# A sliding-window attention backward with a gated MLP: buffers of probability pairs, and six more transposes on TensorE

## The chip, the cores and the metric

The kernel runs on one core of one Trainium2 chip. The metric is the device time of one execution in microseconds (us). A core has TensorE (PE, with its weight loads PEld), VectorE (DVE), ScalarE (ACT), GpSimd (POOL) and SyncE (SP), which here only issues DMAs. Each engine works through its own instructions in order; an instruction waits until the semaphores that it names have been raised. SP's DMAs are issued in order too: one that waits holds up all behind it.

## The reference

The kernel computes a forward pass and the gradients of one layer that mixes two branches by a gate. Cut to what matters (S = 2048 tokens, D = 512, 32 heads of 16, a window of 256 tokens, F = 1376, all bf16):

```python
g = sigmoid((x * gate_w).sum(-1, keepdims=True))
# a: attention, each query sees itself and the 255 tokens before it
scores = einsum("bhqd,bhkd->bhqk", q, k) * Dh ** -0.5     # masked to the window
a = einsum("bhqk,bhkd->bhqd", softmax(scores), v) -> @ wo
# b: gated MLP
b = einsum("bsf,fd->bsd", relu(x @ W_gate) * (x @ W_up), W_down)
out = g * a + (1 - g) * b
# returned: out and the gradients of (out * grad_out).sum() by
# A_x, A_wqkv, A_wo, B_W_gate, B_W_up, B_W_down, gate_w
```

(In the reference `x` of both branches is `A_x`.) For the attention's gradients every score tile is needed twice: as probabilities P, and as P times dP, where dP is the product of the output's gradient with V. Both are needed with keys along the partitions (as they come from the matmul) and with queries along them (transposed).

## The kernel before

The program has three stages.

**MLP, 0 to about 250 us** (lines 186 to 454). The gate's and the MLP's products, forward and backward, in tiles of 128 hidden units by 512 tokens; the results that are needed later are stored to DRAM.

**Attention, about 250 to 775 us** (lines 456 to 897). Heads are worked in four head groups `c` of eight heads (DC = 4), queries in 16 blocks `j` of 128 (NT = 16). A query block meets up to three key blocks: its own (role "d", diagonal, masked above the diagonal), the one before (role "m", middle, no mask) and the one before that (role "f", far, masked). Each meeting is made for two halves of four heads, so a block has six units, and fewer at the start of a head group: two in block 0, four in block 1. The order of the units in a whole block is m, f, d of the first half, then m, d, f of the second (lines 592 to 605). 360 units in all.

One unit goes through these steps, by slot `n` of a loop that issues one unit per slot (lines 809 to 897):

- slot n, `front`: TensorE makes the scores ST (line 616), ScalarE their exponential into Pu (line 627), POOL masks it where the role is d or f (lines 629 and 632). `front_dp`: TensorE makes dPT (line 641).
- slot n+1, `gradp`: VectorE multiplies Pu by dPT into Pd (line 646).
- slot n+2, `flip`, for units with `u.dma` set: a DMA transpose on SP's queue. The two halves of a diagonal pair share one tile PPd (Pu and Pd of both halves, 4 KB per partition), transposed in one DMA into `p2d` (line 671), which is issued two slots after the second half. A first middle unit has a tile PPm of its own (2 KB), transposed into `p2` (line 678).
- slot n+3 (LAG = 3), `rowsum`: TensorE sums rows and the products with K and V into BA (lines 655 and 657), which ScalarE copies out after the block's last unit (line 661). Then `flip` for the other units (second middle and far ones): TensorE transposes Pu and Pd in eight pieces (line 687), and a copy takes them out of PSUM, by ScalarE and VectorE in turn (`copier`, `evac`, lines 72 and 74).
- Some slots after a block's end: `small_ops` (lines 692 to 726), a division on VectorE and eight small operations on POOL; and later still `cd_piece` (lines 478 to 490), which uses the transposed tiles as weights for the gradients of K and V.

All of ST, dPT and the projections' results rotate through four PSUM tiles of one tag "M". PPd has two buffers, PPm three, Pu and Pd (of units that are flipped on TensorE) three each. A buffer of PPd or PPm is free again when its DMA transpose has landed and its `rowsum` is done.

Besides its own work the loop spreads background work by a planner with a running credit: the projections of the next group of four blocks (`project_parts`), among them `tr_rows`, a DMA transpose on SP's queue into one of two buffers `rows` (line 171), whose former content is read last by POOL's small operations (lines 709 to 716); the loads of the masked layout `z` (line 468); the weight gradients of the head group before (line 572); and in the last groups the loads and transposes of the weights of the last stage (`plan`, lines 517 and 527), all on SP's queue. A unit that is flipped on TensorE takes 0.44 from the credit (line 863).

**Output, from about 775 us on** (lines 907 to 1003). For each of 16 token blocks the output, the gradient of x and pieces of other gradients, from operands that are loaded from DRAM in eight groups of two blocks.

Of the kernel before, what the change touches and what calls it, by code (L numbers as in the profile page):

```python
# [11 lines left out]
BF = mybir.dt.bfloat16  # L12
# [10 lines left out]
def kernel(  # L23
# [21 lines left out]
    P = 128  # L45
# [10 lines left out]
    DC = D // P  # L56
# [55 lines left out]
    if True:  # L112
        HH = HG // 2
# [74 lines left out]
    with ExitStack() as p1, tc.manual_schedule():  # L188
# [33 lines left out]
        half = TPG // 2  # L222
# [234 lines left out]
    if True:  # L457
# [4 lines left out]
        wk = p3b.enter_context(tc.tile_pool(name="attw", bufs=2))  # L462
# [130 lines left out]
        for c in range(DC):  # L593
            for j in range(NT):
                kbs = [k for k in (j - 1, j, j - 2) if k >= 0]
                for half in range(2):
                    order = kbs if half or len(kbs) < 3 else [kbs[0], kbs[2], kbs[1]]
                    for ki, kb in enumerate(order):
                        u = Unit()
                        u.c, u.j, u.kb, u.half = c, j, kb, half  # L600
                        u.first = ki == 0 and half == 0
                        u.last = ki == len(kbs) - 1 and half == 1
                        u.role = ("d", "m", "f")[j - kb]
                        u.dma = u.role == "d" or (u.role == "m" and half == 0)
                        units.append(u)
        NU = len(units)

        pairs = {}

        def front(u):  # L610
            tg, jl = u.j // TPG, u.j % TPG
            z = zt[(u.c * NTG + tg) % ZB]
            KTt = proj[(u.c, u.kb // TPG)][f"K{u.half}"]
            ksl = slice((u.kb % TPG) * P, (u.kb % TPG + 1) * P)
            ST = ps.tile([P, HH, P], F32, tag="M", bufs=4, name="ST")
            nc.tensor.matmul(ST[:], lhsT=KTt[:, ksl], rhs=z[:, 0, jl, :, :], start=True, stop=True)  # L616
            if u.role == "d":
                if u.half == 0:
                    pairs[(u.c, u.j)] = wk.tile([P, 2, 2, HH, P], BF, tag="PPd", bufs=2, name="PPd")
                u.PP = pairs[(u.c, u.j)][:, u.half, :, :, :]  # L620
                u.Pu, u.Pd = u.PP[:, 0, :, :], u.PP[:, 1, :, :]
            elif u.dma:
                u.PP = wk.tile([P, 2, HH, P], BF, tag="PPm", bufs=3, name="PPm")
                u.Pu, u.Pd = u.PP[:, 0, :, :], u.PP[:, 1, :, :]
            else:
                u.Pu = wk.tile([P, HH, P], BF, tag="Pu", bufs=3, name="Pu")
            nc.scalar.activation(u.Pu[:], ST[:], ACT.Exp)  # L627
            if u.role == "d":
                nc.gpsimd.affine_select(out=u.Pu[:], in_=u.Pu[:], compare_op=ALU.is_ge, fill=0.0, base=0,  # L629
                                        pattern=[[0, HH], [1, P]], channel_multiplier=-1)  # L630
            elif u.role == "f":
                nc.gpsimd.affine_select(out=u.Pu[:], in_=u.Pu[:], compare_op=ALU.is_ge, fill=0.0, base=-1,  # L632
                                        pattern=[[0, HH], [-1, P]], channel_multiplier=1)
# [147 lines left out]
        with tc.manual_schedule():  # L781
# [27 lines left out]
            while n <= NU + LAG or ev or cdq or bgq:  # L809
                now = ev.pop(n, [])  # L810
                u = units[n] if n < NU else None
# [3 lines left out]
                if u is not None:  # L815
                    gi = u.c * NTG + u.j // TPG
                    if u.first and u.j == 0:
                        sts[u.c] = st.tile([P, NT, 4, P], BF, tag="rows_st", name="rows_st")
                    if u.first and u.j % TPG == 0:
                        if gi + 1 < len(groups):  # L820
                            prq = project_parts(*groups[gi + 1])
                            due = n + sum(2 * min(3, j + 1) for j in range(u.j, u.j + TPG)) - 3
                            if gi + 2 == len(groups):
                                due -= 10
                    if u.first and u.j == 6 and u.c > 0:
                        ev.setdefault(n + 1, []).append(("dma", lambda c=u.c - 1: spill(c, NT // 2)))
                    if u.first and u.j == 1 and u.c > 0:
                        ready = grad_parts(u.c - 1)
                    if u.first and u.j == TPG - 1 and u.c > 0:
                        bgq += ready  # L830
                    front(u)
                    if u.last and gi + 1 == len(groups) and u.j % TPG in (1, 3):
                        ev.setdefault(n + 2, []).append(("dma", lambda i=(u.j % TPG) // 2: early_f(i)))
# [200 lines left out]
```

## Time and profile before

| what | us |
|---|---|
| median of 3 runs | 970.24 |
| lowest and highest | 968.97, 972.31 |
| the profiled execution, its own time | 972.45 |
| its span, first to last instruction | 970.7 |
| mean granted TensorE clock | 0.987 of full |

The page gives the busy time of each engine, a strip of the span in 40 slices and a chain of waits that ended last. A row of the timeline gives an instruction's start in us from the span's start, its length, engine, line, operation, tiles written and read, shapes, and in brackets the idle time of the engine before it with what ended that idle time. "SPq" rows are DMA issues on SP's queue: start, and how long the issue occupied the queue; the transfer lands later. A row of the waits reads: who waited, for whom, total us, number of times, longest.

### The profile page before, as it was taken

The numbers are of one execution on the slowest core, as the hardware profiler recorded it, in microseconds if no ns is written. First come the engines' busy times: TensorE is split into PE (matmuls) and PEld (weight loads), VectorE is DVE, ScalarE is ACT, GpSimd is POOL, SyncE is SP. The second block draws the span as 40 slices with busy tenths as digits, with TensorE's granted clock in tenths as the row PEclk, the third lists the DMA queues.
The fourth block names the chain that finished last, engine by engine and source line by source line (L and its number), as shares of the span: only waits on it lengthen the run. The fifth ranks groups of instructions, "written<-read, shape, count | busy, mean of one in ns | idle before, by whom it ended". The sixth has DMA issues, their size and how long they took to land.

```text
span 970.7 us, 26875 instructions
## 1 busy us (share of the span) xinstructions
PE 928.5 (96%) x11017; PEld 588.2 (61%) x11017; DVE 501.0 (52%) x918; ACT 456.6 (47%) x792; POOL 487.0 (50%) x935
## 2 busy tenths in 40 slices
PE   8999999999899998999998999989998999999998
PEld 5555655656567765677765777756776644444443
DVE  4443334334477776567765676756676322223223
ACT  5423222223367876667775667756676410000001
POOL 2644545444267766656766567765676511112211
PEclk9999999999999999999998999989999999999999
DMA  9988989998578985698969879979999899777751
GB/s 295 185 195 180 200 190 211 206 223 199 118 125 136 152 156 106 114 166 129 163 109 131 161 112 183 140 133 158 170 168 197 172 244 233 193 188 192 187 104 45
DMA packets 477172, 161.86 MB, mean 167 GB/s; under 512 B 405784, under 2 KB 474744, under 8 KB 477048
## 3 DMA queue, kind: packets, MB, share of 16 engines
q1 hardware_dynamic: 454648, 137.06, 76.2%
q10 hardware_dynamic: 20592, 17.84, 6.5%
q0 software_dynamic: 1808, 5.24, 1.6%
q8 instruction: 86, 1.41, 0.6%
q14 instruction: 38, 0.31, 0.1%
HBM read 32.15 MB, written 36.31 MB: 71 GB/s over the span
## 4 chain that ended last, share of the span: by engine, by line
PE 69%; DMA 10%; POOL 7%; DVE 6%; ACT 3%; issue 3%; SPq 1%; POOLq 0%; ACTq 0%; DVEq 0%
PE dxps L976 7%; PE wps L371 6%; PE ST L616 6%; PE pt L687 5%; PE dPT L641 5%; PE wps L572 4%; PE dxps L991 4%; DMA p2d<-PPd 4%; PE pp L128 4%; PE bps L945 3%; PE dhps L324 3%; PE dps L373 3%; PE ups L324 3%; PE gps L324 3%; PE BA L655 3%
## 5 line engine op out<-in xcount | busy, mean ns | idle before, releaser
L641 PE MATMUL dPT<-z,V 128*128 128x512 bf16 x360 | 138.6, 385 | 13.9 <-ACT PPd L627 10.8
L646 DVE TENSOR_TENSOR Pd<-Pu,dPT 128x512 bf16<-128x512 bf16 x172 | 116.7, 679 | 64.4 <-POOL Pu L632 51.1
L616 PE MATMUL ST<-z,K 128*128 128x512 bf16 x360 | 138.4, 384 | 8.0 <-ACT PPd L627 2.5
L627 ACT ACTIVATE Pu<-ST 128x512 bf16<-128x512 f32 x172 | 104.1, 605 | 47.5 <-PE ST L616 39.5
L629 POOL TENSOR_SCALAR_AFFINE_SELECT PPd<-PPd 128x512 bf16<-128x512 bf16 x128 | 81.6, 637 | 85.9 <-ACT PPd L627 85.5
L646 DVE TENSOR_TENSOR PPd<-PPd,dPT 128x512 bf16<-128x512 bf16 x128 | 87.5, 683 | 56.5 <-POOL PPd L629 55.0
L338 POOL TENSOR_TENSOR hT<-rg,upm 128x512 bf16<-128x512 bf16 x44 | 51.4, 1167 | 118.7 <-DVE upm L336 82.6
L371 PE MATMUL wps<-dgu_r,x_r 128*128 128x256 bf16 x704 | 105.6, 273 | 0.9 <-DVE wst L74 0.9
L627 ACT ACTIVATE PPd<-ST 128x512 bf16<-128x512 f32 x128 | 77.1, 602 | 51.3 <-PE ST L616 28.9
L72 ACT COPY p<-pt 128x1024 bf16<-128x1024 bf16 x86 | 87.6, 1019 | 4.8 <-PE pt L687 2.4
L371 PEld LDWEIGHTS <-x_r 128*128 128x128 bf16 x704 | 68.8, 98 | 32.2 <-issue 1.4
L632 POOL TENSOR_SCALAR_AFFINE_SELECT Pu<-Pu 128x512 bf16<-128x512 bf16 x112 | 71.4, 638 | 27.7 <-ACT Pu L627 27.4
L954 ACT COPY a_sb<-aps 128x512 f32<-128x512 f32 x16 | 9.4, 586 | 154.9 <-issue 139.7
L336 DVE SCALAR_TENSOR_TENSOR upm<-rg,ups 128x512 bf16<-128x512 bf16 x44 | 30.2, 686 | 81.7 <-ACT rg L330 42.1
L486 PE MATMUL CD<-rq,p 128*128 128x32 bf16 x928 | 68.4, 177 | 0.0
L330 ACT ACTIVATE rg<-gps 128x512 bf16<-128x512 f32 x44 | 26.3, 598 | 88.8 <-PE gps L324 43.0
L687 PE MATMUL pt<-ident,Pd 128*128 128x128 bf16 x688 | 67.8, 222 | 0.0
L687 PE MATMUL pt<-ident,Pu 128*128 128x128 bf16 x688 | 67.2, 220 | 0.0
L489 PEld LDWEIGHTS <-p 128*128 128x128 bf16 x928 | 54.8, 96 | 20.2 <-issue 1.1
L373 PE MATMUL dps<-db_r,h_r 128*128 128x512 bf16 x176 | 66.7, 379 | 0.0
L489 PE MATMUL CD<-rq,p 128*128 128x16 bf16 x928 | 66.7, 169 | 0.0
L486 PEld LDWEIGHTS <-p 128*128 128x128 bf16 x928 | 62.1, 96 | 1.2 <-issue 1.1
(167 smaller groups left out, 2250.4 us busy)
## 6 DMA issues: line engine op xcount, KB each, us to landing
dqkvo_d<-rows_st SPq DMA_DIRECT2D x7, 1024.0 KB, 6.3
hT_d<-hT ACTq DMA_DIRECT2D x44, 128.0 KB, 2.6
dgT_d<-dgu ACTq DMA_DIRECT2D x44, 128.0 KB, 3.0
duT_d<-dgu ACTq DMA_DIRECT2D x44, 128.0 KB, 3.1
duT_g<-duT_d SPq DMA_DIRECT2D x8, 640.0 KB, 5.7
gt<-hT_d SPq DMA_DIRECT2D x7, 640.0 KB, 5.8
dgT_g<-dgT_d SPq DMA_DIRECT2D x7, 640.0 KB, 5.0
z<-zT SPq DMA_DIRECT2D x60, 64.0 KB, 2.2
```

The source lines that it names most:

```text
L72: nc.scalar.copy(out, in_)
L324: nc.tensor.matmul(out[:], lhsT=w(c), rhs=x(c), start=(c == 0), stop=(c == DC - 1))
L371: nc.tensor.matmul(acc["w"][:, c, :], lhsT=x_r[:, t, c * P:(c + 1) * P], rhs=k.dgu_r[:, :, i, :], start=(go_ and c % 2 == 0), stop=no_, sk ...
L373: nc.tensor.matmul(acc["d"][:], lhsT=k.h_r[:, i, :], rhs=db_r[:, t, :], start=go_, stop=no_)
L486: nc.tensor.matmul(cd[0][:, h, :], lhsT=p2[:, 0, hh, :], rhs=rq[:, h, 0:2 * Dh], start=cd[1], stop=True, skip_group_check=True)
L489: nc.tensor.matmul(cd[0][:, h, 0:Dh], lhsT=p2[:, 1, hh, :], rhs=rq[:, h, 2 * Dh:3 * Dh], start=False, stop=True, skip_group_check=True)
L616: nc.tensor.matmul(ST[:], lhsT=KTt[:, ksl], rhs=z[:, 0, jl, :, :], start=True, stop=True)
L627: nc.scalar.activation(u.Pu[:], ST[:], ACT.Exp)
L629: nc.gpsimd.affine_select(out=u.Pu[:], in_=u.Pu[:], compare_op=ALU.is_ge, fill=0.0, base=0, pattern=[[0, HH], [1, P]], channel_multiplier=-1)
L641: nc.tensor.matmul(u.dPT[:], lhsT=VTt[:, ksl], rhs=z[:, 1, jl, :, :], start=True, stop=True)
L646: nc.vector.tensor_tensor(out=u.Pd[:], in0=u.Pu[:], in1=u.dPT[:], op=ALU.mult)
L687: nc.tensor.transpose(pt[:, a, hh, :], src[:, hh, :], ident[:])
```

## The change

Three edits. PPd gets a third buffer (4 KB more per partition). PPm gets two buffers instead of three (2 KB less). And the first middle units of the last head group, in blocks 10 to 15, no longer have `u.dma` set: these six units are flipped on TensorE, one slot later, with their Pu and Pd in the tiles of the tags Pu and Pd and not in PPm.

```diff
@@ -601,7 +601,7 @@
                         u.first = ki == 0 and half == 0
                         u.last = ki == len(kbs) - 1 and half == 1
                         u.role = ("d", "m", "f")[j - kb]
-                        u.dma = u.role == "d" or (u.role == "m" and half == 0)
+                        u.dma = u.role == "d" or (u.role == "m" and half == 0 and (c < DC - 1 or j < 10))
                         units.append(u)
@@ -616,11 +616,11 @@
             if u.role == "d":
                 if u.half == 0:
-                    pairs[(u.c, u.j)] = wk.tile([P, 2, 2, HH, P], BF, tag="PPd", bufs=2, name="PPd")
+                    pairs[(u.c, u.j)] = wk.tile([P, 2, 2, HH, P], BF, tag="PPd", bufs=3, name="PPd")
                 u.PP = pairs[(u.c, u.j)][:, u.half, :, :, :]
                 u.Pu, u.Pd = u.PP[:, 0, :, :], u.PP[:, 1, :, :]
             elif u.dma:
-                u.PP = wk.tile([P, 2, HH, P], BF, tag="PPm", bufs=3, name="PPm")
+                u.PP = wk.tile([P, 2, HH, P], BF, tag="PPm", bufs=2, name="PPm")
                 u.Pu, u.Pd = u.PP[:, 0, :, :], u.PP[:, 1, :, :]
```

## The prediction

> **What bounds the kernel now.** I read the page first: which engine is full, and what the chain of waits runs through.
>
> ```profile
> span 970.7 us, 26875 instructions
> ...
> PE 928.5 (96%) x11017; PEld 588.2 (61%) x11017; DVE 501.0 (52%) x918; ACT 456.6 (47%) x792; POOL 487.0 (50%) x935
> ...
> PE   8999999999899998999998999989998999999998
> ...
> PE 69%; DMA 10%; POOL 7%; DVE 6%; ACT 3%; issue 3%; SPq 1%; POOLq 0%; ACTq 0%; DVEq 0%
> ```
>
> TensorE is busy for 96% of the span, and in nearly every slice of it (a digit is a fortieth, in tenths), so the time can only fall where it idles or runs slowly, and every instruction added to it counts. One foreign thing stands on the chain, the DMA `p2d<-PPd`, the transpose of a diagonal pair. The view of waits says what it holds up (columns: total us, times, longest):
>
> ```profile
> ACT PPd L627 <- DMA p2d<-PPd: 19.1, 8, 4.0
> ...
> PE dPT L641 <- ACT PPd L627: 10.8, 6, 3.8
> PE ST L616 <- ACT PPd L627: 2.5, 2, 2.1
> PE dPT L641 <- DVE Pd L646: 2.3, 2, 1.4
> PE BA L655 <- ACT BAs L661: 2.2, 1, 2.2
> ```
>
> ScalarE's exponential into PPd waits until the transpose out of that buffer has landed, because there are only two; TensorE then waits for ScalarE, 13.3 us in the second and third rows. The timeline of TensorE gives the places (in brackets: idle time before, and what ended it):
>
> ```profile
> 387.62 0.59 PE L641 MATMUL dPT<-z,V 128*128 128x512 bf16 x1 [3.39 <-ACT PPd L627]
> ...
> 517.43 0.19 PE L655 MATMUL BA<-KV,PPm 128*128 128x33 bf16 x1 [2.19 <-ACT BAs L661]
> ...
> 633.42 0.38 PE L616 MATMUL ST<-z,K 128*128 128x512 bf16 x1 [2.07 <-ACT PPd L627]
> ...
> 648.77 0.59 PE L641 MATMUL dPT<-z,V 128*128 128x512 bf16 x1 [2.22 <-ACT PPd L627]
> ...
> 750.62 0.38 PE L641 MATMUL dPT<-z,V 128*128 128x512 bf16 x1 [3.77 <-ACT PPd L627]
> ```
>
> Around or right behind each of these five gaps the clock drops. The view by windows shows it (columns: length, busy time and count of PE, PEld, DVE, ACT, POOL; clock; DMA share; GB/s):
>
> ```profile
> 385.90:392.70 6.80, 5.08 (x76) 3.43 (x76) 2.05 (x4) 3.96 (x7) 3.91 (x10) 0.50 1.09 165
> 515.60:522.40 6.80, 4.96 (x74) 3.58 (x74) 3.12 (x6) 3.55 (x7) 4.29 (x10) 0.50 0.96 166
> 635.10:638.40 3.30, 3.30 (x23) 1.86 (x22) 1.87 (x3) 2.05 (x4) 0.04 (x1) 0.50 0.31 58
> 648.70:652.10 3.40, 3.33 (x52) 2.50 (x52) 1.45 (x4) 2.25 (x5) 2.68 (x7) 0.50 1.27 120
> 751.10:754.50 3.40, 3.40 (x50) 2.30 (x47) 2.00 (x4) 2.45 (x4) 2.40 (x7) 0.50 0.98 202
> ```
>
> In 20.1 us of work at half clock, half, 10.0 us, is lost. So a late transpose costs twice: the gap, and the slow stretch behind it.
>
> **Part one: a third PPd buffer.** A buffer is reused two blocks later now, three blocks later then. Away from the head-group boundaries (385, 515 and 647 us) nothing else stands close. Of the 10.8 us, 3.39 and 2.22 lie at boundaries, which leaves 5.2; the 2.5 us of ST lie outside too. With half of the two slow stretches outside (3.30 and 3.40, so 3.35) this is 5.2 + 2.5 + 3.35 = **11.0 us gained**. What is late next there is POOL's masking, and it has room:
>
> ```profile
> 638.91 0.64 POOL L629 TENSOR_SCALAR_AFFINE_SELECT PPd<-PPd 128x512 bf16<-128x512 bf16 x1 [3.76 <-ACT PPd L627]
> ...
> 750.64 0.64 POOL L629 TENSOR_SCALAR_AFFINE_SELECT PPd<-PPd 128x512 bf16<-128x512 bf16 x1 [4.09 <-ACT PPd L627]
> ```
>
> **The boundaries** are another matter. Blocks 0 and 1 of a head group have only 2 and 4 units, so small operations of three blocks crowd on POOL, and SP's queue falls behind at the transpose of rows (line 171), which waits for POOL's last reader of an older buffer. First the queue's own waits, then the timelines of SP, ACT and POOL at the first boundary:
>
> ```profile
> SPq L171 <- POOL rows_st L716: 31.0, 8, 5.2
> ```
> ```profile
> 382.42 2.15 SPq L671 DMA_TRANSPOSE p2d<-PPd  x1
> ...
> 386.25 1.28 SPq L678 DMA_TRANSPOSE p<-PPm  x1
> ```
> ```profile
> 386.97 0.60 ACT L627 ACTIVATE PPd<-ST 128x512 bf16<-128x512 f32 x1 [3.40 <-DMA p2d<-PPd]
> ...
> 392.75 0.60 ACT L627 ACTIVATE PPm<-ST 128x512 bf16<-128x512 f32 x1 [0.63 <-PE ST L616]
> ```
> ```profile
> 387.64 0.63 POOL L629 TENSOR_SCALAR_AFFINE_SELECT PPd<-PPd 128x512 bf16<-128x512 bf16 x1 [1.63 <-ACT PPd L627]
> ```
>
> POOL idled only 1.63 us there, so the mask comes at most that much earlier, not 3.40. And this is where **part two, PPm from three buffers to two**, costs something. The unit at 392.75 will reuse the buffer whose transpose is issued at 386.25, behind L171 and others in SP's order, none of which waits for the PPd that we free. Its landing takes, from the view of the tile PPm:
>
> ```profile
> L678 SPq DMA_TRANSPOSE p<-PPm x60: 1231/1274/3973, 264.5 to 763.1; - x60
> ...
> DMA to landing us min/median/max: 3.1/4.2/8.4
> ```
>
> 386.25 + 4.2 = 390.45, so this unit gains at most 2.3 us before the new wait holds it. Behind it on ScalarE stand the next exponentials and the copy of BAs, and TensorE waits for those. The other two boundaries:
>
> ```profile
> 515.69 1.28 SPq L678 DMA_TRANSPOSE p<-PPm  x1
> ```
> ```profile
> 521.90 0.60 ACT L627 ACTIVATE PPm<-ST 128x512 bf16<-128x512 f32 x1 [0.62 <-PE ST L616]
> ```
> ```profile
> 648.79 0.64 POOL L629 TENSOR_SCALAR_AFFINE_SELECT PPd<-PPd 128x512 bf16<-128x512 bf16 x1 [0.47 <-ACT PPd L627]
> ...
> 650.34 0.20 POOL L708 TENSOR_TENSOR ndel<-BAs,rinv 128x8 f32<-128x8 f32 x1 [0.55 <-DVE rinv L705]
> ```
>
> At the second 515.69 + 4.2 = 519.9 against 521.90: 2.0 us. At the third POOL is the tightest, with 0.47 + 0.55 = 1.0 us of idle time. Together **5.3 us gained**. The bounds: nothing, if the new waits trip the half clock again; everything, 3.39 + 2.2 + 2.22 = 7.8 us of gaps and half of 5.08 + 4.96 + 3.33, 6.7 us, so 14.5. I take the caps because they come from issues and masks whose order the change leaves alone.
>
> The Trainium skill, "TensorE: Matmul & The Clock Gate", section "HAM oscillation — how this bites in real kernels", has the clock fall only after idle gaps of more than about 3.4 us. The rows above differ: single gaps of 2.07 and 2.22 us were followed by a half-clock stretch. By the page the shorter waits that I leave at the boundaries would cost no clock, and the sum stands; by the rows each that stays above 2.07 us would cost another 1.7 us, 5.1 us for three.
>
> Elsewhere the two PPm buffers have room, but little at some places. The tightest that stays:
>
> ```profile
> 326.14 1.26 SPq L678 DMA_TRANSPOSE p<-PPm  x1
> ```
> ```profile
> 332.06 0.60 ACT L627 ACTIVATE PPm<-ST 128x512 bf16<-128x512 f32 x1 [0.24 <-PE ST L616]
> ```
>
> 326.14 + 4.2 = 330.3, about 1.7 us before the use two blocks on. I cost it at nothing: the landing comes before the use. If that cover goes, the wait is as long as the landing is late, and rival 3 begins.
>
> **Part three: six middle units on TensorE.** Blocks 10 to 15 of the last head group, first half: six DMA transposes go, each of 1.2 to 4.0 us of SP's queue by the row of L678 above; six flips come, each of eight transposes and one copy, alternately by ACT and DVE. The order of everything else in the planner stays the same (it loses 0.44 of credit per flip, but no later piece moves). Their price, from the chain of waits in order of time, and from the view of the tile pt:
>
> ```profile
> 763.73 0.46 PE pt L687 x8
> ```
> ```profile
> L72 ACT COPY p<-pt x86: 1007/1012/1042, 264.4 to 761.8; 128x1024 bf16<-128x1024 bf16 x86
> L74 DVE COPY p<-pt x86: 676/683/692, 269.3 to 764.2; 128x1024 bf16<-128x1024 bf16 x86
> ```
> ```profile
> 720.00:757.00 37.00, 32.38 (x628) 24.26 (x625) 23.45 (x42) 25.62 (x44) 26.11 (x60) 0.95 1.03 192
> ```
>
> 6 x 0.46 = **2.8 us added**, all on the bound engine. The copies lie beside it: ACT has 11.4 of 37 us free, DVE 13.5, and three copies take 3.0 and 2.1. If instead each flip cost a whole ACT copy it would be 6 x 1.01 = 6.1; if TensorE's small remaining gaps took it in, nothing. The freed SP time, 7 to 24 us, helps the pair transposes of that stretch, which part one already counts. Pu and Pd, three buffers each, now serve four units of a block instead of three, reused after four units at the nearest; the flip runs three units later and ahead of the next ST on TensorE's own order, so no new wait.
>
> **The sum.** -11.0 - 5.3 + 2.8 = -13.5 us. The profiled execution, 972.45 us with a span of 970.7, would become 958.9; it lies 2.2 us above the median of the runs, 970.24, and from the median **956.7 us** follows. The later stage starts 13.5 us earlier and has TensorE full in every slice (the last nine digits above), so nothing is given back.
>
> **Rivals.** (1) The boundaries recover fully, because SP and POOL catch up while TensorE is no longer stopped: 970.24 - 11.0 - 14.5 + 2.8 = 947.5. For it: POOL is idle a quarter of the stretch from 720 on (26.11 of 37). Against it: the landing at 390.45, which SP's order fixes. (2) The boundaries give nothing and the flips cost their copies: 970.24 - 11.0 + 6.1 = 965.3. For it: ACT and DVE together with masks form the loop that feeds TensorE. Against it: their free time in the window. (3) Slower: the two PPm buffers become the new wait at group transitions, where L171 stops SP (eight waits in the row above). Each would cost a gap of 2.1 us and 1.7 us of half clock, 3.8 us. From four such places on (15.2 us) the gain of 13.5 is gone; at seven of the fourteen transitions with DMA units it is 970.24 - 13.5 + 26.6 = 983.3. It needs landings some 2 us later than now. Against it: no ScalarE wait for a PPm transpose has a row now, and the margin of 1.7 us above. (4) The stalls hide behind a DMA limit (its share is 1.03 from 720 on) and the landings just come later: no change, 970. Against it: in that stretch six transposes are taken away.
>
> **How the numbers follow.** Forecast 0.60, rival 1 0.20, rival 2 0.10, rival 3 0.06, rival 4 0.04. 0.3% of the time, 2.9 us, is about what the measurement can tell from no change. The first three are faster, 0.90; rival 4 is the same, 0.04; rival 3 slower, 0.06. The range reaches from rival 1 with free flips (944.7) to rival 2: 945 to 965.
>
> **What would show it.** Right: no row in which ACT's PPd waits for p2d for over 1 us; no half clock near 632 and 750 us; new waits of ACT's PPm for its DMA just behind the head-group boundaries, 1 to 2 us each; 712 transposes of Pu and 712 of Pd at L687, six units of four more than in the trace of before; the last stage as long as before. Wrong: waits of PPm at ordinary group transitions, half clock at new places, or p2d waits that persist, which would mean that SP's lateness exceeds three blocks.

## The result, and the profile after

| | before | changed |
|---|---|---|
| median of the runs beside each other, us | 970.86 | 954.33 |
| lowest and highest, us | 968.97, 972.31 | 954.09, 954.86 |
| ratio, 95% interval | | 0.9832 [0.9813, 0.985] |
| span of the profiled execution, us | 970.7 | 952.6 |
| its granted clock | 0.987 | 1.0 |

The change makes the kernel 16.5 us faster; 13.5 had been forecast. First the page of the changed kernel, with the rows that answer to those of before:

```profile
span 952.6 us, 26867 instructions
PE 917.2 (96%) x10965; PEld 586.9 (62%) x11065; DVE 503.1 (53%) x921; ACT 458.6 (48%) x795; POOL 486.9 (51%) x935
...
PE   7999999999989999999999999989999999999998
...
PEclk9999999999999999999999999999999999999999
...
PE 65%; POOL 11%; DMA 7%; DVE 6%; issue 5%; ACT 3%; SPq 2%; ACTq 0%; POOLq 0%; DVEq 0%
```

TensorE's row can't be compared with the one before as it stands: 100 records of matmuls are missing from this trace. A second trace of the same kernel, from its run again at the end of the experiments, has them all, 48 more than before, as six flips of eight transposes make:

```profile
PE 924.1 (97%) x11065; PEld 587.6 (62%) x11065; DVE 500.7 (53%) x921; ACT 458.7 (48%) x795; POOL 485.6 (51%) x935
```

There TensorE is busy for 4.4 us less than before, though work was added to it: a matmul at half clock takes longer. The DMA's share of the chain fell from 10% to 7% and POOL's rose from 7% to 11%. Now the waits of the changed kernel, first ScalarE's within the attention stage, then TensorE's:

```profile
ACT PPd L627 <- PE ST L616: 31.4, 51, 1.9
...
ACT PPm L627 <- DMA p<-PPm: 2.1, 2, 1.5
ACT PPm L627 <- PE CD L489: 2.0, 1, 2.0
```
```profile
PE pp L131 <- DVE zT L140: 3.0, 7, 0.4
PE dPT L641 <- DVE Pd L646: 2.3, 2, 1.4
PE ST L616 <- DVE Pd L646: 2.0, 4, 1.0
PE dPT L641 <- DVE PPd L646: 1.9, 6, 0.6
```

The row of ScalarE's PPd waiting for `p2d<-PPd`, 19.1 us before, is gone, and with it both rows of TensorE waiting for ScalarE's PPd, 13.3 us. In their place stand three waits for PPm, 4.1 us together. The waits for VectorE that now lead TensorE's list were in large part there before (the second row with the same 2.3 us).

Where the time came from can be read block by block. The start of the copy of BAs (line 661) at a block's end, 64 of them in each trace, is subtracted, before minus changed:

| stretch, head group and block | gain at its start | at its end | gained | forecast |
|---|---|---|---|---|
| first head group, one wait and the start | -0.32 | 0.45 | 0.8 | 0.75 |
| first boundary, 1/0 to 1/2 | 0.45 | 3.54 | 3.1 | 2.3 |
| second boundary, 1/15 to 2/2 | 3.49 | 7.91 | 4.4 | 0.39 + 2.0 = 2.4 |
| 2/12 to 3/2, with the third boundary | 7.88 | 13.26 | 5.4 | 0.66 + 2.07 + 1.65 + 1.0 = 5.4 |
| 3/9 to 3/15, the last PPd wait less the flips | 13.23 | 15.95 | 2.7 | 3.77 + 1.7 - 2.8 = 2.7 |

Between these stretches the gain stays constant to some hundredths, so nothing else moved. The sum, 15.95 + 0.32 = 16.3 us, lies close to the 16.5 us between the medians. (The 0.32 us is time that the trace of the changed kernel lost ahead of the attention stage.) The spans differ by 18.1: 15.95 up to the end of the attention stage, 1.75 more by one wait of 1.9 us that the profiled execution of before had in the last stage (TensorE's bps for VectorE's amb) and no later trace has, and 0.4 in the last microseconds, where the trace of before alone ran at half clock.

### The profile page after: what moved, and what is told of

Its sections match the earlier page's. It is cut to its first block, busy times and chain, and to the rows that moved or that the text cites. A ratio compares the mean times of both kernels' runs of the same rounds, so it can differ in the third digit from the quotient of the medians.

```text
span 952.6 us, 26867 instructions
## 1 busy us (share of the span) xinstructions
PE 917.2 (96%) x10965; PEld 586.9 (62%) x11065; DVE 503.1 (53%) x921; ACT 458.6 (48%) x795; POOL 486.9 (51%) x935
## 4 chain that ended last, share of the span: by engine, by line
PE 65%; POOL 11%; DMA 7%; DVE 6%; issue 5%; ACT 3%; SPq 2%; ACTq 0%; POOLq 0%; DVEq 0%
PE dxps L976 7%; PE pt L687 5%; PE ST L616 5%; PE wps L371 5%; PE dPT L641 5%; PE dxps L991 4%; PE wps L572 4%; PE pp L128 4%; PE bps L945 4%; POOL Pu L632 3%; PE dhps L324 3%; PE BA L655 3%; PE CD L486 2%; PE gps L324 2%; PE ups L324 2%
## 5 line engine op out<-in xcount | busy, mean ns | idle before, releaser
L646 DVE TENSOR_TENSOR Pd<-Pu,dPT 128x512 bf16<-128x512 bf16 x178 | 120.2, 678 | 62.2 <-POOL Pu L632 49.7
L616 PE MATMUL ST<-z,K 128*128 128x512 bf16 x354 | 133.7, 378 | 6.1 <-DVE Pd L646 2.0
L641 PE MATMUL dPT<-z,V 128*128 128x512 bf16 x348 | 131.5, 378 | 4.4 <-DVE Pd L646 2.3
L627 ACT ACTIVATE Pu<-ST 128x512 bf16<-128x512 f32 x178 | 107.6, 604 | 45.4 <-PE ST L616 35.3
L72 ACT COPY p<-pt 128x1024 bf16<-128x1024 bf16 x89 | 90.7, 1019 | 7.5 <-PE pt L687 4.9
L74 DVE COPY p<-pt 128x1024 bf16<-128x1024 bf16 x89 | 60.8, 684 | 6.0 <-PE pt L687 5.9
```

What stands on the lines that cost most here:

```text
L72: nc.scalar.copy(out, in_)
L641: nc.tensor.matmul(u.dPT[:], lhsT=VTt[:, ksl], rhs=z[:, 1, jl, :, :], start=True, stop=True)
L646: nc.vector.tensor_tensor(out=u.Pd[:], in0=u.Pu[:], in1=u.dPT[:], op=ALU.mult)
```

## The experiments

Each time is a median on one chip beside runs of the kernel before on the same chip, and the ratio is to those; the chips differ between experiments (the kernel before took 970.0 to 971.5 us on them), so differences of a microsecond are read from the traces. Of the kernel with stalls put in there is one run. Room in SBUF is short: where PPd and PPm both have three buffers, or rows has three beside three PPd, Pu and Pd were cut to two. That cut alone was not tried; the next two experiments bear on it.

**One part at a time.** Three PPd, with PPm left at three and no flips:

```diff
-tag="PPd", bufs=2 ... tag="PPm", bufs=3 ... tag="Pu", bufs=3 ... tag="Pd", bufs=3
+tag="PPd", bufs=3 ... tag="PPm", bufs=3 ... tag="Pu", bufs=2 ... tag="Pd", bufs=2
```

> Three PPd buffers, PPm left at three, no flips moved (Pu and Pd go from three buffers to two to make room; without the moved units each is reused after four units, behind its flip in TensorE's own order). Theory: in the changed kernel the two-buffer PPm made ScalarE wait 2.0, 0.6 and 1.5 us at the three head-group boundaries, but POOL's crowd of small operations ends there at almost the same moment, so without the PPm waits at most 1.5 us comes back; the 2.8 us of flips come back too, and SP stays as loaded in the last blocks as before. Expected 951 to 955. Rival, the PPm waits are on the path in full: 4.1 us less than the changed kernel and the flips' 2.8 less, 947 to 948. Second rival, the flips were needed for SP: 957 or more, with waits of PPd for its transpose after 700 us.

954.36 us, ratio 0.9832 [0.982, 0.9845], the same as the changed kernel. No wait for a PPm transpose is left, and the first boundary gains 3.1 us just as with two PPm buffers: 0.64 to 3.75 by the copies of BAs. So taking the PPm waits away alone gains nothing there, though they are real. The second boundary gave 1.0 us less than in the changed kernel, for another reason (the clock, below).

The change without its third part:

```diff
-tag="PPd", bufs=2 ... tag="PPm", bufs=3
+tag="PPd", bufs=3 ... tag="PPm", bufs=2
```

> The change without its third part: three PPd, two PPm, all first middle units transposed by DMA. Theory (flips cost TensorE 2.8 us; without them the two PPm buffers wait some 0.5 to 1.5 us in blocks 12 to 15 of the last head group, since one landing of before came 0.5 us after its buffer's use two blocks on): 952 to 954, the changed kernel's 954.3 or up to 2 us below it. Rival (the freed SP time is what removes the last stall): ScalarE waits of 2 us or more for PPm or PPd after 720 us, half clock behind them, 957 to 960.

953.05 us, 0.9818 [0.9805, 0.9831]. Theory held, with 4 PPm waits in place of 2:

```profile
ACT PPm L627 <- DMA p<-PPm: 5.4, 4, 1.9
```

None of them costs more than a few tenths by the copies of BAs. This kernel has three Pu and Pd, and it gains the same as the one above at the first and third boundary (3.1 and 5.4 us in both), so the cut to two shows no cost. The attention stage ends 1.1 us earlier than in the changed kernel, so the six flips cost some 1.1 to 1.2 us there, and with three PPd buffers they buy nothing: the last wait is removed twice.

The flips alone (the first hunk of the diff), and two PPm buffers alone:

> The third part alone: PPd two, PPm three buffers, six flips on TensorE. Theory (SP is issuing back to back from 728 to 752 us, so six transposes less let the pair's transpose land in time): the 3.8 us gap and the half clock at 750 us go, 5.5 us, the flips cost 2.8: 967.5 to 969. All stalls before 700 us stay. Rival (that pair is late for another reason): 2.8 us slower than before, 973 to 974.

967.46 us, 0.997 [0.9957, 0.9983]. Theory: the wait at 750 us is gone, and ScalarE's waits for `p2d<-PPd` fall to

```profile
ACT PPd L627 <- DMA p2d<-PPd: 16.3, 8, 3.7
```

From block 12 to 13 of the last head group 3.6 us are gained. So six transposes less on SP's queue do let the pair land in time; the third part is a cure of its own for one stall.

> The second part alone: PPd two, PPm two buffers, no flips. Theory: with PPd's waits still there every PPm landing but one comes before its use, so 970 to 972.5, with one new wait of about 0.5 us near 743 us. Rival (two PPm buffers are themselves a bound at group transitions): 975 or more, with waits of PPm for its transpose outside the last blocks.

971.06 us, 1.0009 [0.9997, 1.0021]; one PPm wait of 0.5 us. As expected.

**What the slow clock cost.** The kernel before, its stalls kept and filled with transposes of the identity:

```diff
+        FILL = {(99, "dp"): 54, (189, "dp"): 22, (189, "ba"): 36, (271, "st"): 32, (279, "dp"): 36, (351, "dp"): 60}
+        def fill(n, at):
+            if (n, at) in FILL:
+                pt = ps.tile([P, 2, HH, P], BF, tag="TR", name="fill")
+                for i in range(FILL[(n, at)]):
+                    nc.tensor.transpose(pt[:, i // HH % 2, i % HH, :], ident[:], ident[:])
...
+                    fill(n, "st")
                     front(u)
...
+                    fill(n, "dp")
                     front_dp(u)
                     pieces()
+                    fill(n, "ba")
```

> The kernel before with its stalls left in, and transposes of the identity that nobody reads put in TensorE's order just where it stalls: 54 ahead of dPT at 384 us, 22 and 36 around dPT at 513 us, 32, 36 and 60 at 631, 647 and 747 us, each a little less than the stall that it fills. The clock should stay at full. Theory, formed after the first four runs (what came back at each place was nearly the gap itself, 15.4 us of gaps for some 17 us, so the slow clock behind a gap cost little, since POOL and ScalarE set the pace there): 968 to 971. Rival, the prediction's reckoning (half of 20.1 us of work is lost): 960 to 962.

968.16 us, 0.997 [0.9957, 0.9982], 2.6 us by the medians. In the attention stage 3.8 us come back by the copies of BAs (from 0.26 at its start to 4.06). Of the five slow stretches four are gone; the one that is left has its own gap, where the wait had moved beyond the filler. The windows and TensorE's timeline of this kernel, and ScalarE's waits:

```profile
646.80:650.20 3.40, 3.17 (x52) 2.25 (x51) 1.33 (x3) 2.48 (x5) 3.11 (x8) 0.50 1.06 182
```
```profile
645.20 0.38 PE L641 MATMUL dPT<-z,V 128*128 128x512 bf16 x1 [2.88 <-ACT PPd L627]
```
```profile
ACT PPd L627 <- DMA p2d<-PPd: 18.3, 7, 4.9
```

The stalls kept nearly their sum (19.1 us before) but not their places: at the second boundary and at the last stall they became shorter, at the third longer. The first boundary is the cleanest: the wait is 3.3 us against 3.4, and 1.6 us come back, where half of the 5.08 busy us would be 2.5. Taken together the slow clock of the four stretches that went cost some 4 us, not the 8.4 of the prediction's reckoning, and the rival falls; since waits moved, the size for a single place stays open.

The changed kernel with stalls of chosen length put in:

```diff
             nc.scalar.activation(u.Pu[:], ST[:], ACT.Exp)
+            for _ in range(AGAIN.get((u.c, u.j), 0) if u.role == "m" and u.half == 1 else 0):
+                nc.scalar.activation(u.Pu[:], ST[:], ACT.Exp)
...
+        AGAIN = {(1, 5): 3, (1, 8): 5, (1, 11): 7, (1, 14): 9, (2, 5): 4, (2, 8): 6, (2, 11): 8, (2, 13): 10}
```

> The changed kernel with ScalarE's exponential of one unit repeated, which changes no value, to make stalls of chosen length at quiet places: 3, 5, 7 and 9 times in blocks 5, 8, 11 and 14 of the second head group, 4, 6, 8 and 10 times in blocks 5, 8, 11 and 13 of the third, some 0.5 us for each. Shows which gaps of TensorE are followed by half clock, and what a block loses beside the gap. Theory (from the trace of before: 2.07 us was followed by half clock, 1.23 and 1.89 were not): half clock behind every gap of over 2.1 us. Rival (the page of the skill): only behind gaps of over 3.4 us. Loss of time in total 20 to 30 us.

985.4 us, 31 more than the changed kernel and so a little beyond the 20 to 30 that were expected. Its timeline of TensorE has the gaps, its windows the stretches at half clock:

```profile
443.82 1.02 PE L128 MATMUL pp<-x,p 128*128 128x512 bf16 x3 [1.95 <-ACT Pu L630]
...
470.29 0.58 PE L617 MATMUL ST<-z,K 128*128 128x512 bf16 x1 [3.81 <-ACT Pu L630]
...
585.06 1.49 PE L128 MATMUL pp<-x,p 128*128 128x512 bf16 x3 [3.30 <-ACT Pu L630]
...
635.61 0.59 PE L617 MATMUL ST<-z,K 128*128 128x512 bf16 x1 [5.16 <-ACT Pu L630]
```
```profile
469.40:476.30 6.90, 5.79 (x57) 3.41 (x58) 3.25 (x6) 3.75 (x7) 3.16 (x7) 0.51 0.78 100
500.10:503.60 3.50, 3.24 (x38) 2.14 (x38) 2.04 (x4) 2.70 (x5) 2.61 (x6) 0.51 0.04 7
585.50:588.90 3.40, 3.40 (x24) 1.47 (x24) 2.04 (x5) 1.08 (x2) 2.45 (x6) 0.50 0.34 66
612.80:616.20 3.40, 3.26 (x36) 2.12 (x37) 2.08 (x4) 1.76 (x3) 3.15 (x7) 0.50 0.31 56
633.30:640.10 6.80, 4.49 (x55) 2.83 (x55) 3.26 (x5) 5.09 (x9) 3.21 (x7) 0.50 0.90 171
```

| gap, us | half clock behind it, us | time lost by the block, us |
|---|---|---|
| 1.95 | none | 2.3 |
| 3.30 | 3.4 | 4.9 |
| 3.50 | 3.4 | 4.5 |
| 3.81 | 6.8 | 6.4 |
| 4.10 | 3.4 | 5.1 to 5.2 |
| 5.16 | 6.8 | 6.7 |

The stalls of three and four repeats left no gap above 0.75 us. A gap of 3.30 us trips the clock and one of 1.95 does not; with 2.07 from before, the rival of 3.4 us is out. Beyond the gap the five tripped blocks lost 1.0 to 2.6 us, 7.7 together, against half of their busy time at half clock, 10.1. Even in quiet blocks half of the busy time is more than was lost, taken together.

**What makes the pairs late, and what holds the boundaries now.** The kernel before with a third buffer for rows (Pu and Pd as they were):

```diff
-rows = pjA.tile([P, 2, TPG, P], BF, tag="rows", bufs=2, name="rows")
+rows = pjA.tile([P, 2, TPG, P], BF, tag="rows", bufs=3, name="rows")
```

> The kernel before with a third buffer for rows in place of the whole change, so that the transpose of rows at line 171 no longer waits for POOL's last read of an older buffer. Theory (at the head-group boundaries this wait is what makes the pair's transpose late): the PPd waits at 387, 516 and 648 us go, the ones at 626, 633 and 750 us stay: some 8 to 10 us faster than before, 961 to 963. Rival (SP is late for its load of transfers, not for this wait): 969 or more.

958.32 us, 0.9873 [0.9856, 0.989]: better than expected. SP's queue at the first boundary of this kernel, against 379.54 for L171 before:

```profile
374.31 1.23 SPq L171 DMA_TRANSPOSE rows<-zT  x1
...
376.98 3.17 SPq L671 DMA_TRANSPOSE p2d<-PPd  x1
```

The wait of SP for POOL's `rows_st`, 31.0 us before, is gone, and of ScalarE's 19.1 us

```profile
ACT PPd L627 <- DMA p2d<-PPd: 7.3, 4, 4.1
```

are left. The wait of L171 was the cause at all three boundaries and, against my expectation, of TensorE's waits at 626 and 633 us as well. Of the large ones only the stall before the last blocks stays, the one that the flips alone remove:

```profile
738.02 0.58 PE L641 MATMUL dPT<-z,V 128*128 128x512 bf16 x1 [3.80 <-ACT PPd L627]
```

Three PPd, two PPm, no flips, and three rows on top:

> Three PPd, two PPm, no flips moved, and a third buffer for rows (Pu and Pd two buffers each to make room). Theory (the PPm waits at the boundaries cost nothing because POOL's crowd ends there at the same moment): the PPm waits shrink and the time stays, 952 to 954, as without the third rows buffer. Rival (they are on the path): 949 to 950.

953.31 us, 0.983 [0.9815, 0.9846]: theory, the boundaries gain nothing more.

POOL's part, on the kernel without flips:

```diff
-            return (..., (s + 6, "pool", pool3), (s + 7, "pool", pool4))
+            lag = {0: 5, 1: 3}.get(j, 0)
+            return (..., (s + 6 + lag, "pool", pool3), (s + 7 + lag, "pool", pool4))
```

> Three PPd, two PPm, no flips moved, and of POOL's small operations those that make the gradient of Q (lines 719 to 723, some 1.25 us for a block) five slots later for block 0 and three slots later for block 1 of a head group, out of the crowd at the boundary. Theory (POOL's crowd is what holds the boundaries now): the gaps of TensorE there, 0.5 + 0.6, 1.4 and 0.5 + 0.6 us, shrink, and blocks 1 to 2 of the second to fourth head group come 1 to 1.5 us earlier each: 949 to 951. Rival (the late landings for the two PPm buffers hold the boundaries): the same waits of PPm as before, longer by what POOL gives, and 952.5 to 954.

953.38 us, 0.9801 [0.978, 0.9822]; by the ratios 1.7 us better than without POOL's part, which is within the intervals; neither theory alone. The start of the first head group comes 1.1 us earlier and the third boundary 0.7, but the first only 0.1: there TensorE now waits for the exponential into PPm, which waits for its buffer (the transpose landed at 388.71 us, the exponential began at 388.80),

```profile
389.44 0.38 PE L616 MATMUL ST<-z,K 128*128 128x512 bf16 x1 [0.70 <-ACT PPm L627]
```

and the second lost 1.0 us to half clock. So both were tried away together, three PPm and POOL's operations later:

> Three PPd, three PPm (Pu and Pd two each), no flips moved, and POOL's small operations of blocks 0 and 1 later, as in the run before. Theory (at the boundaries two things end within a few tenths of each other, POOL's crowd and the landing for the third PPm user, so that taking one away alone gave nothing at the first boundary): with both away the first and third boundary come 1 to 2 us earlier than with either alone, no PPm wait for a DMA is left, 950.5 to 952.5. Rival (something third, TensorE's own work, ends there too): 953 to 954.5.

950.6 us, 0.9803 [0.979, 0.9817], beside the changed kernel's 953.62, 0.9831 [0.9818, 0.9845], on the same chip. The first boundary gains 0.9 us over the kernel with neither, where three PPm alone gave 0.0 and POOL alone 0.1; the third gains 0.9, after 0.0 and 0.7. At the first boundary two limits lay on top of each other, as the theory has it, though what taking both away gave lies just under the 1 to 2 us expected; at the third POOL's alone was most of it. This version beats both kernels; its last blocks still need no flips.

**What a flip costs.** Fifteen first middle units of the second head group flipped on TensorE, on the kernel without flips:

```diff
-u.dma = u.role == "d" or (u.role == "m" and half == 0)
+u.dma = u.role == "d" or (u.role == "m" and half == 0 and c != 1)
```

> Three PPd, two PPm, and the fifteen first middle units of the second head group flipped on TensorE. Shows what a flip costs in ordinary blocks. Theory of the prediction (TensorE is the bound, a flip costs its eight transposes): 15 x 0.46 = 6.9 us more than without, 959 to 961, spread over all blocks. Rival (from the changed kernel, whose six flips cost 1.1 us against the same kernel without them: other engines set part of the pace): 15 x 0.19 = 2.8 us more, 955 to 957, most of it in blocks with background work on TensorE.

956.75 us, 0.9843 [0.9828, 0.9858], 3.7 us more than the 953.05 without, which were measured on another chip; by the ratios 2.4 us more. Over that head group the copies of BAs fall back by 3.9 us against the trace without: 0.26 us for a flip, about half of its eight transposes' 0.46. By the traces the truth lies between the two, nearer to the rival.

**The changed kernel again:**

> The changed kernel itself once more, on the same chip as the run beside it. 953.5 to 955 on the theory that its third part costs 1.1 us against the same kernel without it (953.05).

953.62 us, as expected. Its trace has a stretch of half clock at the second boundary, which the first trace of the same kernel lacks.

## Why the prediction was right, and where its sizes were off

**The stall and its cure: right.** Every wait of PPd for its transpose is gone and so is every slow stretch in the attention stage of the first trace; 712 transposes of Pu and of Pd, as forecast, and the last stage unchanged but for the one wait and the 0.4 us at its end named above. The wait at 633 us, which the prediction put outside the boundaries, is that of the last head group's first block; it went with the others.

**The new PPm waits: right in place and nearly in size, wrong in what they meant.** SP, ScalarE and POOL of the changed kernel at the first boundary, then ScalarE at the others:

```profile
385.55 1.31 SPq L678 DMA_TRANSPOSE p<-PPm  x1
```
```profile
390.09 0.60 ACT L627 ACTIVATE PPm<-ST 128x512 bf16<-128x512 f32 x1 [2.01 <-PE CD L489]
...
514.45 0.60 ACT L627 ACTIVATE PPm<-ST 128x512 bf16<-128x512 f32 x1 [0.63 <-DMA p<-PPm]
...
640.41 0.60 ACT L627 ACTIVATE PPm<-ST 128x512 bf16<-128x512 f32 x1 [1.49 <-DMA p<-PPm]
```
```profile
385.52 0.64 POOL L629 TENSOR_SCALAR_AFFINE_SELECT PPd<-PPd 128x512 bf16<-128x512 bf16 x1
```

Three waits of 0.6 to 2.0 us, just behind the boundaries, with the first exponential at 390.09 where 390.45 had been worked out. (The first row names PE's CD as the releaser; the trace gives the landing of the transpose issued at 385.55 as 390.01, and that is what it waited for.) And POOL's mask of the diagonal follows the work ahead of it without a gap, where it had idled 1.63 us. But the step "together 5.3 us gained" took the shift of one late exponential for the shift of the block, and here the term was mis-sized. At the first boundary the exponential came 2.2 us earlier beside the 0.45 already won, and the block's end 3.1: the other 0.9 us were made up within the block, whose next exponential began 1.07 us behind this one (391.16), where before it had been 1.95 (394.70). With three PPm buffers the gain was the same 3.1.

**The second boundary: the landing was not fixed.** The prediction had no issue ahead of PPm's transpose waiting for the PPd that is freed. SP's queue in the changed kernel:

```profile
503.76 1.23 SPq L171 DMA_TRANSPOSE rows<-zT  x1
...
511.02 1.28 SPq L678 DMA_TRANSPOSE p<-PPm  x1
```

PPm's transpose is issued 4.7 us earlier than before (515.69), while the block had gained only 3.5 when it entered the boundary; 1.2 us are the queue's own. The landing then took 3.4 us in place of the 4.2 reckoned with (issued at 511.02, landed at 514.37), another 0.8. L171 waits for POOL's operations of the block before, and before, these had stood behind a wait of ScalarE for PPd of 1.5 us at 506 us, of which the prediction counted only the 0.39 us that TensorE lost by it. With 4.4 us gained for 2.4 this is 2.0 of the miss of 2.8 us that the table shows; the first boundary is the rest.

**The half clock: too dear, and so were the flips.** The prediction took half of the busy time in a slow stretch. The filled kernel got 3.8 us back for the four stretches that it removed, where that rule has 8.4. The factor is not the same everywhere: from 2/12 to the first block of the last head group, with the waits at 626 and 633 us, 4.05 us came back, where the gaps and half of the stretch behind them make 4.4. At the last stall the error was hidden: 3.77 + 1.7 - 2.8 = 2.7 came out to the tenth, but without flips those blocks gained 4.0, hardly more than the gap, and the flips took 1.2; that it came out was luck. Both terms assumed a TensorE that is the only bound. It is busy in every slice, yet slower by half its clock it lost less than half, and with 0.46 us more to do for a flip it lost 0.26; so part of the pace must be set elsewhere. That it is POOL, VectorE and ScalarE, whose waits for each other fill the waits' list, is argued and not shown for each place.

**The rivals.** Full recovery at the boundaries (947.5) did not come: it counted 6.7 us of half clock there alone, where the four stretches of the filled kernel cost some 4. That the flips cost a whole ACT copy, that two PPm buffers bind at ordinary group transitions (971.06 alone, with one PPm wait of 0.5 us, at 742 us in the last blocks) and that DMA simply lands later are refuted.

**The rule on the clock.** The Trainium skill, "TensorE: Matmul & The Clock Gate", section "HAM oscillation — how this bites in real kernels", has gaps over about 3.4 us lower the clock. The trace disagrees: 2.07, 2.22, 2.88 and 3.30 us did it too.

## What to carry to other kernels

When a rotating buffer is released by a DMA, look for the DMA that stands ahead of it in its queue and for what that one waits for: here one third buffer for rows gave 12.4 of the 16.5 us without touching the pairs. Price a stall by its gap and treat a slow clock behind it as a bound on more, not as a sum. And where taking one limit away gives nothing, look for a second that ends at the same moment before calling the first harmless.

## What the hardware showed that was not expected

A gap of 1.4 us can lower the clock, or not. The second boundary leaves TensorE idle for 1.38 to 1.40 us, by VectorE's multiplication behind POOL's crowd, in nine of the traces; in five of them 3.4 us of half clock follow, in four nothing does. The changed kernel is on both sides: nothing in its first trace, a slow stretch in its second. The same window in the kernel with three PPd and three PPm, and in the changed kernel:

```profile
510.70:514.10 3.40, 3.40 (x61) 2.57 (x60) 2.43 (x5) 1.03 (x3) 2.77 (x8) 0.52 0.92 175
```
```profile
510.70:514.10 3.40, 3.33 (x79) 2.68 (x80) 2.12 (x5) 1.49 (x3) 2.78 (x8) 1.00 0.78 145
```

It costs about 0.9 to 1.0 us where it happens. All stretches in the attention stage last 3.4 or 6.8 us, and the traces' record of the granted clock shows that within a trace they begin on one grid. Before, they begin at 385.87, 515.58, 635.04, 648.70 and 751.10 us, which lie 38, 35, 4 and 30 steps of 3.413 us apart; every other trace with more than one stretch keeps to such a grid too. What seems to count is how much of a step TensorE idles, and so where the gap falls in it. The steps around the gap, two of the changed kernel's first trace (counted back from its only stretch, at the program's end) and the one of its second:

```profile
506.49:509.91 3.42, 2.41 (x52) 1.84 (x52) 1.71 (x4) 3.16 (x6) 3.26 (x11) 1.00 0.99 133
509.91:513.32 3.41, 2.67 (x61) 2.13 (x61) 2.62 (x5) 1.10 (x4) 2.71 (x8) 1.00 0.82 163
```
```profile
507.16:510.57 3.41, 1.91 (x39) 1.11 (x37) 1.41 (x3) 2.54 (x5) 3.25 (x9) 1.00 1.19 134
```

In the first the end of a step cuts the gap in two, in the second the gap lies within one step, and half clock begins with the next. (In the kernel with three PPd, two PPm and no flips it lies within one step as well, with 1.38 us of idle time in all, and nothing follows.) In the five traces of which no matmul record is missing, every step at full clock in the attention stage with 1.50 us or more of idle time was followed by half clock, and none with 1.15 or less. It is not the whole rule: in the kernel with stalls put in, a step with some 1.7 us of idle time, that of the 1.95 us gap, was not followed by it. This was read off the traces; no run was made to test it. By it the half clock from 515.58 us on at the second boundary of the kernel before belongs rather to the gap of 1.39 us just ahead than to the one of 2.19 us, which had only begun.

And transposes that nobody reads are enough to keep the clock up: where they filled the gap, no slow stretch followed.
